# An earlier warm-up from a small cleared tile, a new order for the first four blocks, and copies moved to ScalarE

## The chip, the cores and the metric

One core of one Trainium2 chip. The metric is the device time of one execution in microseconds (us). Executions of a kernel are compared in runs of the state that the measurements call fast; the one run of 3364.69 us in the control, marked slow, is left out. What the state doesn't separate is how long TensorE ran at half clock; each run also lists its mean granted TensorE clock (the share of full speed that the chip let it run at, 1.0 or 0.5 in every record of these traces), and that turns out to matter here.

In the lines of the profile PE is TensorE, PEld its weight loads, DVE VectorE, ACT ScalarE, POOL GpSimd, and SP the queue that issues transfers (DMA). The span goes from the first to the last instruction of the profiled execution. L260 is line 260 of the kernel.

## The reference

```python
# B, H, S, D = 4, 8, 768, 48; all float32
for t in range(S):
    state = alpha[:, :, t, :, None] * state + einsum('bhd,bhde->...', k[:, :, t], v[:, :, t])   # outer product
    y[:, :, t] = einsum('bhd,bhde->bhe', q[:, :, t], state)
x = y.transpose(0, 2, 1, 3).reshape(3072, 384)
h = np.maximum(x @ w_in, 0.0)          # w_in 384 x 2048, float64 in memory
out = (h * h @ w_out).astype(np.float32)
```

(The einsum of the outer product is shortened here.) The recurrence is computed in blocks of 128 time steps: 24 blocks, four at a time as a group. A block takes logs of alpha (step `ln`), their running sums by a product with a triangle of ones (`cs`), exponentials of the sums and their inverse (`eb`, `ei`), scales q and k with them (`mq`, `mk`), turns both with TensorE (`qT`, `kT`), copies them out of PSUM, the memory that the program lets TensorE write to, in tiles called banks here (`qc`, `kc`), forms scores (`sc`), masks them (`am`), and makes outputs (`y`, `ev`) and the next state (`kv`, `st`).

## The kernel before

The steps of the first four blocks are written out in a string, in the order in which every engine gets its instructions. In the timelines each engine works through its own in that order (TensorE, before: `kT0` at 9.55 us, `qT0` at 10.02, `cs1` at 10.49, `sc0` at 11.33), so the place of a step decides what it can be held up by.

```python
    s_t = kept("s", B, [128, NP, 64])          # states, cleared by GpSimd after q and k tiles
    for t in s_t:
        nc.gpsimd.memset(t, 0.0)
    ...
    am_t = kept("am", NAM, [128, 2, NP, 128])  # masked scores, cleared by VectorE
    for t in am_t:
        nc.vector.memset(t, 0.0)
    ...
    def warm(_):
        nc.tensor.matmul(
            out=ps_att.tile([128, NP, C], FP32, tag="att", name="warm"),
            lhsT=am_t[1][:, 0, 0, :], rhs=am_t[1][:, 0], start=True, stop=True,
        )
    warm(0)
    warm(0)
    ...
    VECTOR = ("k0", "k1", "k2", "k3", "q1", "q2", )
    def copied(x, n):                          # steps kc and qc
        t = blk[n][f"{x}s"] = work(f"{x}s", 2)
        copy = nc.vector.tensor_copy if f"{x}{n}" in VECTOR else nc.scalar.copy
        copy(out=t, in_=blk[n].pop(f"{x}T"))
    ...
    first = """
        ln0 load0v warm0 cs0 ei0 eb0 mk0 mq0 load2a load2q load2k bl0 ln1 kT0 kc0 load1v
        qT0 qc0 cs1 load3a sc0 weights0 load3q load3k eb1 mq1 load2v bl1 ei1 mk1 kT1 kc1
        qT1 qc1 am0 kv0 ln2 br0 cs2 ei2 eb2 sc1 am1 mq2 bl2 load3v mk2 br1
        weights1 ln3 y0 ev0 kT2 kc2 qT2 qc2 kv1 cs3 ei3 eb3 mk3 weights2 first0 st0
        mq3 load4q load4k load4v kT3 middle0 sc2 kc3 bl3 qT3 second0 qc3 am2 br3 br2 st1
        kv2 sc3 am3 ha0 weights3 load4a ha1 first1 middle1 y2 ev2 second1 st2 hb0 first2 hb1
        kv3 middle2 st3
    """
```

`first`, `middle` and `second` are the three parts of turning a float64 weight tile into float32, on VectorE, ScalarE and VectorE. `ha` and `hb` are the first feed-forward products. Everything behind this string (the feed-forward network and the other 20 blocks) is some 535 us long and unchanged.

Of the kernel before, what the change touches and what calls it, by code (L numbers as in the profile page):

```python
# [8 lines left out]
FP32 = mybir.dt.float32  # L9
# [14 lines left out]
def kernel(  # L24
# [25 lines left out]
    nc = tc.nc  # L50
    B, H, S, D = q.shape
    C = 128
    NCH = S // C
    NP = H // 2
# [14 lines left out]
    ps_att = ctx.enter_context(tc.tile_pool(name="ps_att", bufs=4, space=PSUM))  # L69
# [4 lines left out]
    def kept(name, n, shape):  # L74
        return [consts.tile(shape, FP32, name=f"{name}{i}") for i in range(n)]

    NV = 3
    tiles = {
        "a": kept("a_in", 2, [128, H * D]), "q": kept("q_in", 2, [128, H, 64]),
        "k": kept("k_in", 4, [128, H, 64]), "v": kept("v_in", NV, [128, H * D]),  # L80
    }
# [1 line left out]
        nc.gpsimd.memset(t[:, :, D:64], 0.0)  # L83

    tiles["w"] = kept("vx_in", 2, [128, H // 2 * D])
    s_t = kept("s", B, [128, NP, 64])
    for t in s_t:
        nc.gpsimd.memset(t, 0.0)

    NW = 8  # L90
    w_in = [consts.tile([128, KM, DF // NW], FP32, name=f"w_in{i}") for i in range(NW)]
# [4 lines left out]
    def flat(t):  # L96
        return t.rearrange("a x y -> a (x y)")
# [4 lines left out]
    for n in (2, 3):  # L102
        t = lent["q", n] = flat(w_out[4 + n])[:, 0 : 64 * H].rearrange("a (h d) -> a h d", h=H)
# [104 lines left out]
    am_t = kept("am", NAM, [128, 2, NP, 128])  # L208
# [21 lines left out]

    def warm(_):
        nc.tensor.matmul(  # L232
            out=ps_att.tile([128, NP, C], FP32, tag="att", name="warm"),
            lhsT=am_t[1][:, 0, 0, :], rhs=am_t[1][:, 0], start=True, stop=True,
        )

    warm(0)
    warm(0)


    blk = [{} for _ in range(NBLK)]
# [8 lines left out]
    def work(name, bufs=1):  # L250
        return p2.tile([128, NP, C], FP32, tag=name, name=name, bufs=bufs)
# [59 lines left out]
        turned("k", n)  # L311


    VECTOR = ("k0", "k1", "k2", "k3", "q1", "q2", )

    def copied(x, n):
        t = blk[n][f"{x}s"] = work(f"{x}s", 2)
        copy = nc.vector.tensor_copy if f"{x}{n}" in VECTOR else nc.scalar.copy
        copy(out=t, in_=blk[n].pop(f"{x}T"))
# [88 lines left out]
    def y(n):  # L408
# [50 lines left out]
        for phase in range(2):  # L459
# [20 lines left out]
            for m in ns:  # L480
# [5 lines left out]
                for p in range(NP):  # L486
                    half = slice(64 * (p % 2 ^ phase), 64 * (p % 2 ^ phase) + 64)
                    for e in range(2):
# [3 lines left out]
                            lhsT=tiles["k"][m % 4][half, 2 * p + e, :],  # L492
                            rhs=tiles["v"][m % NV][half, first : first + 64],
                            start=(p % 2, e) not in begun, stop=True, skip_group_check=True,
# [209 lines left out]
    def ffn_product(g, i, r):  # L704
# [68 lines left out]
    steps["hb"] = lambda j: ffn_in(0, j, slice(HT, 2 * HT))  # L773
    steps["first"], steps["middle"], steps["second"] = convert_first, convert_middle, convert_second
    first = """
        ln0 load0v warm0 cs0 ei0 eb0 mk0 mq0 load2a load2q load2k bl0 ln1 kT0 kc0 load1v
        qT0 qc0 cs1 load3a sc0 weights0 load3q load3k eb1 mq1 load2v bl1 ei1 mk1 kT1 kc1
        qT1 qc1 am0 kv0 ln2 br0 cs2 ei2 eb2 sc1 am1 mq2 bl2 load3v mk2 br1
        weights1 ln3 y0 ev0 kT2 kc2 qT2 qc2 kv1 cs3 ei3 eb3 mk3 weights2 first0 st0
        mq3 load4q load4k load4v kT3 middle0 sc2 kc3 bl3 qT3 second0 qc3 am2 br3 br2 st1  # L780
        kv2 sc3 am3 ha0 weights3 load4a ha1 first1 middle1 y2 ev2 second1 st2 hb0 first2 hb1
        kv3 middle2 st3
    """
    for word in first.split():
        f = max((x for x in steps if word.startswith(x)), key=len)
# [97 lines left out]
```

## Time and profile before

| | before |
|---|---|
| time, three runs | 580.06, 583.12, 583.3 us |
| profiled execution | 579.81 us, span 577.9 us |
| first feed-forward product (`ha`) | 31.69 us |
| first products of full width (128x512) | 42.31 us |
| TensorE's waits, all | 9.8 us |
| clock from 20.65 to 31.69 us | 0.69 of full speed |

Read it from the back: from 42.31 us on TensorE is full, so the change can only move that moment. The lines are in the prediction.

### The profile page before, as it was taken

To read this page: it belongs to the slowest core of one execution; us is meant where nothing else is said; L and a number is where in the kernel's file an instruction comes from. 1 tells how busy PE (TensorE), PEld (TensorE's weight loads), DVE (VectorE), ACT (ScalarE), POOL (GpSimd) and SP (SyncE) were. 2 spreads that over 40 slices of the span, in tenths; PEclk is the share of its full clock that TensorE was granted. 3 is DMA by queue.
4 is the path that set the end of the run, shared out by engine and by line. 5 is a ranking of instruction groups with operands and counts; after the bars stand their busy time and mean duration, and the time that the engine had idled before them with its cause. 6 is when DMAs were issued, how large, how long until landed. Compare 5 with 4: busy or idle time off the path is not lost.

```text
span 577.9 us, 11428 instructions
## 1 busy us (share of the span) xinstructions
PE 563.1 (97%) x4754; PEld 481.8 (83%) x4754; DVE 330.1 (57%) x657; ACT 220.8 (38%) x489; POOL 4.5 (1%) x29
## 2 busy tenths in 40 slices
PE   6789999999999999999999999999999999999996
PEld 3664555677889999889999889999988999988996
DVE  3888949875784634564544565552566443366430
ACT  3457966433334423333252333342333432333100
POOL 3000000000000000000000000000000000000000
PEclk9899999999999999999999999999999999999999
DMA  9886457623001535000445100424300340100001
GB/s 165 217 194 204 110 139 230 148 33 85 0 1 30 95 59 124 1 0 14 73 85 102 37 1 1 83 57 90 77 1 1 56 68 1 56 1 1 1 1 55
DMA packets 127963, 38.94 MB, mean 67 GB/s; under 512 B 119700, under 2 KB 122792, under 8 KB 127912
## 3 DMA queue, kind: packets, MB, share of 16 engines
q1 hardware_dynamic: 127912, 38.22, 30.2%
q8 instruction: 37, 0.61, 0.4%
q14 instruction: 14, 0.11, 0.1%
HBM read 33.45 MB, written 4.75 MB: 66 GB/s over the span
## 4 chain that ended last, share of the span: by engine, by line
PE 96%; DVE 2%; issue 1%; ACT 0%; POOLq 0%
PE h L649 33%; PE o L720 32%; PE o L686 7%; PE h L611 7%; PE y L416 5%; PE cs L260 3%; PE sc L349 3%; PE kT L303 2%; PE qT L303 2%; PE kv L490 1%; PE warm L232 1%; DVE xT L514 1%; PE sc L335 1%; PE kv L393 1%; DVE am L210 0%
## 5 line engine op out<-in xcount | busy, mean ns | idle before, releaser
L649 PE MATMUL h<-xT,w_in 128*128 128x256 f32 x480 | 124.0, 379 | 0.0
L649 PEld LDWEIGHTS h<-xT,w_in 128*128 128x128 f32 x480 | 91.1, 190 | 12.4
L720 PE MATMUL o<-w_out,hid 128*128 128x192 f32 x480 | 83.3, 327 | 0.0
L720 PEld LDWEIGHTS o<-w_out,hid 128*128 128x128 f32 x480 | 78.7, 190 | 3.7
L514 ACT COPY xT<-y 32x256 f32<-32x256 f32 (+2 forms) x132 | 46.2, 365 | 79.3 <-PE y L416 73.8
L662 DVE TENSOR_TENSOR hid<-h,u 128x256 f32<-128x256 f32 x120 | 50.8, 424 | 28.8 <-PE h L649 25.0
L667 ACT ACTIVATE hid<-hid 128x256 f32<-128x256 f32 x40 | 16.7, 417 | 114.6 <-DVE hid L662 114.6
L662 DVE TENSOR_TENSOR u<-h,u 128x256 f32<-128x256 f32 x80 | 33.8, 423 | 35.3 <-PE h L649 22.9
L649 PE MATMUL h<-s3x,ws 128*128 128x256 f32 x160 | 47.6, 379 | 0.0
L384 DVE COPY_PREDICATED am<-parts,sc 128x384 f32<-128x384 uint32 x40 | 20.6, 578 | 45.2 <-PE sc L349 45.1
L611 PE MATMUL h<-xT,w_in 128*128 128x512 f32 (+1 forms) x108 | 43.7, 551 | 1.8 <-ACT xT L514 1.8
L686 PE MATMUL o<-w_out,hid 128*128 128x384 f32 x128 | 42.9, 488 | 0.0
L720 PE MATMUL o<-t,s 128*128 128x192 f32 x240 | 42.4, 328 | 0.0
L649 PE MATMUL h<-s3x,w_in 128*128 128x256 f32 x160 | 41.1, 379 | 0.0
L720 PEld LDWEIGHTS o<-t,s 128*128 128x128 f32 x240 | 39.0, 190 | 1.3
L611 PEld LDWEIGHTS h<-xT,w_in 128*128 128x128 f32 x108 | 19.7, 190 | 20.9 <-issue 16.7
L686 PEld LDWEIGHTS o<-w_out,hid 128*128 128x128 f32 x128 | 23.8, 190 | 15.6
L649 PEld LDWEIGHTS h<-s3x,w_in 128*128 128x128 f32 x160 | 30.4, 190 | 4.1
L649 PEld LDWEIGHTS h<-s3x,ws 128*128 128x128 f32 x160 | 30.4, 190 | 4.1
L720 PE MATMUL o<-t,hid 128*128 128x192 f32 x160 | 27.9, 329 | 0.0
L669 DVE SCALAR_TENSOR_TENSOR hid<-hid 128x512 f32<-128x512 f32 x40 | 27.2, 681 | 0.0
L720 PEld LDWEIGHTS o<-t,hid 128*128 128x128 f32 x160 | 25.8, 190 | 0.3
(110 smaller groups left out, 763.7 us busy)
## 6 DMA issues: line engine op xcount, KB each, us to landing
raw<-in_moe_w_in_dram SPq DMA_DIRECT2D x8, 768.0 KB, 6.6
raw<-in_moe_w_out_dram SPq DMA_DIRECT2D x8, 768.0 KB, 5.9
k_in<-in_k_dram SPq DMA_DIRECT2D x24, 192.0 KB, 4.4
out_dram<-osb SPq DMA_DIRECT2D x24, 192.0 KB, 1.9
v_in<-in_v_dram SPq DMA_DIRECT2D x23, 192.0 KB, 5.1
a_in<-in_alpha_dram SPq DMA_DIRECT2D x22, 192.0 KB, 3.6
q_in<-in_q_dram SPq DMA_DIRECT2D x22, 192.0 KB, 3.9
vx_in<-in_v_dram SPq DMA_DIRECT2D x40, 48.0 KB, 2.5
```

The source lines that it names most:

```text
L260: nc.tensor.matmul(out=ps.rearrange("a p t -> a (p t)")[:, 0 : H * D], lhsT=causal, rhs=blk[n].pop("la"), start=True, stop=True,)
L303: nc.tensor.transpose(out=ps[:, p, :], in_=rows[:, 128 * p : 128 * (p + 1)], identity=ident)
L349: nc.tensor.matmul(out=chunks(ps[e].rearrange("a p t -> a (p t)"), half, p, i), lhsT=ks[rows, p, 64 * i : 64 * (i + 1)], rhs=qs[rows, p, t ...
L384: nc.vector.copy_predicated(out=o, mask=mask.unsqueeze(1).to_broadcast(list(o.shape)), data=data)
L416: ins = nc.tensor.matmul(out=slot(ps)[64 * half : 64 * half + D + G * e, t], lhsT=lhsT, rhs=rhs, start=key not in seen, stop=True, skip_gr ...
L514: copy(out=x[to : to + m, kk, t : t + 2], in_=blk[n]["y"][e][r : r + m, :, p // 2],)
L611: nc.tensor.matmul(out=ps, lhsT=w[:, kk, c0 : c0 + 128], rhs=xT[g][:, kk, cols], start=(kk == 0), stop=(kk == KM - 1),)
L649: nc.tensor.matmul(out=ps, lhsT=a, rhs=b, start=(step.isupper() and i == 0), stop=(i == len(pairs) - 1), skip_group_check=True,)
L662: nc.vector.tensor_tensor(out=o, in0=ps, in1=z, op=ALU.add)
L669: nc.vector.scalar_tensor_tensor(out=h2, in0=h2, scalar=0.0, in1=h2, op0=ALU.max, op1=ALU.mult)
L686: nc.tensor.matmul(out=acc[t][:, 0:DM], lhsT=hid[i][:, j, t * C : (t + 1) * C], rhs=w_out[i][:, j, :], start=(i == 0 and j == 0), stop=(i ...
L720: nc.tensor.matmul(out=acc[k][:, t, :], lhsT=lhs[:, j, t * C : (t + 1) * C], rhs=rhs[:, j, :], start=(first and r + j + t == 0), stop=(r = ...
```

## The change

The intent: the zero products, among which TensorE's clock came up in the trace before (a weight load of 128 columns took 338 ns until the one at 5.78 us, and 191 from 6.62), start sooner, and a new order of the first four blocks closes gaps, with most copies of turned q and k on ScalarE (0.59 us each there in the trace before, 0.69 on VectorE).

```diff
+    s_t = kept("s", B, [128, NP, 64])         # now ahead of the q and k tiles
+    for t in s_t:
+        nc.gpsimd.memset(t, 0.0)
 ...
-            out=ps_att.tile([128, NP, C], FP32, tag="att", name="warm"),
-            lhsT=am_t[1][:, 0, 0, :], rhs=am_t[1][:, 0], start=True, stop=True,
-    warm(0)
-    warm(0)
+            out=ps_att.tile([128, NP, 64], FP32, tag="att", name="warm"),
+            lhsT=s_t[0].rearrange("a p d -> a (p d)")[:, 0:128], rhs=s_t[0], start=True, stop=True,
+    for _ in range(3):
+        warm(0)
 ...
-    VECTOR = ("k0", "k1", "k2", "k3", "q1", "q2", )
+    VECTOR = ("k1", "k2", )
 ...
+        warm0 ln0 load0v cs0 ei0 eb0 mk0 mq0 load2a load2q load2k bl0 ln1 kT0 qT0 kc0
+        load1v qc0 cs1 load3a sc0 load3k eb1 mq1 bl1 qT1 load2v ei1 mk1 weights0 kT1 kc1
+        qc1 kv0 br0 am0 load3q ln2 cs2 ei2 eb2 sc1 am1 bl2 load3v mq2 mk2 ln3
+        weights1 y0 cs3 ev0 br1 kT2 qT2 ei3 kc2 qc2 kv1 eb3 mk3 load4v kT3 first0
+        st0 mq3 weights2 load4q load4k middle0 sc2 kc3 qT3 second0 qc3 bl3 am2 br3 st1 br2
+        kv2 sc3 am3 ha0 first1 ha1 middle1 y2 ev2 load4a hb0 first2 hb1 second1 st2 kv3
+        middle2 st3 weights3
```

(The old string, printed above, is what the new one replaces.)

More of the change, by code (lines that the diff above doesn't have):

```diff
@@ L85 @@
     tiles["w"] = kept("vx_in", 2, [128, H // 2 * D])
-    s_t = kept("s", B, [128, NP, 64])
-    for t in s_t:
-        nc.gpsimd.memset(t, 0.0)
     NW = 8
@@ L775 @@
     first = """
-        ln0 load0v warm0 cs0 ei0 eb0 mk0 mq0 load2a load2q load2k bl0 ln1 kT0 kc0 load1v
-        qT0 qc0 cs1 load3a sc0 weights0 load3q load3k eb1 mq1 load2v bl1 ei1 mk1 kT1 kc1
-        qT1 qc1 am0 kv0 ln2 br0 cs2 ei2 eb2 sc1 am1 mq2 bl2 load3v mk2 br1
-        weights1 ln3 y0 ev0 kT2 kc2 qT2 qc2 kv1 cs3 ei3 eb3 mk3 weights2 first0 st0
-        mq3 load4q load4k load4v kT3 middle0 sc2 kc3 bl3 qT3 second0 qc3 am2 br3 br2 st1
-        kv2 sc3 am3 ha0 weights3 load4a ha1 first1 middle1 y2 ev2 second1 st2 hb0 first2 hb1
-        kv3 middle2 st3
+        warm0 ln0 load0v cs0 ei0 eb0 mk0 mq0 load2a load2q load2k bl0 ln1 kT0 qT0 kc0
[5 more added lines that the diff above has]
+        middle2 st3 weights3
     """
```

## The prediction

> **What bounds the kernel now.** I read the page's bars first, then the chain that ended last, then TensorE's waits, then the busy times cut at the moments where the first four blocks change stage, and last the timeline of the first 45 us.
>
> The page's bars, 40 slices of 14.4 us:
>
> ```profile
> span 577.9 us, 11428 instructions
> PE 563.1 (97%) x4754; PEld 481.8 (83%) x4754; DVE 330.1 (57%) x657; ACT 220.8 (38%) x489; POOL 4.5 (1%) x29
> ...
> PE   6789999999999999999999999999999999999996
> ...
> PEclk9899999999999999999999999999999999999999
> ...
> PE 96%; DVE 2%; issue 1%; ACT 0%; POOLq 0%
> ```
>
> TensorE is full from the fourth slice to the last, and the chain is TensorE for 96%. The feed-forward products behind it are untouched by this change. What can be won lies in slices one to three, where the bars are 6, 7 and 8 and one slice of clock shows 8. TensorE's waits are all there:
>
> ```profile
> PE warm L232 <- DVE rebias L228: 3.1, 1, 3.1
> PE kT L303 <- DVE k_in L278: 3.0, 3, 1.3
> PE h L611 <- ACT xT L514: 1.8, 3, 1.3
> PE cs L260 <- DVE ks L319: 1.7, 1, 1.7
> PE y L416 <- DVE am L371: 0.2, 1, 0.2
> ```
>
> 9.8 us in all (3.1 + 3.0 + 1.8 + 1.7 + 0.2), each column: total, times, longest. The stages, with busy times, granted clock, DMA share and GB/s:
>
> ```profile
> 0.00:9.55 9.55, 5.23 (x8) 2.11 (x9) 2.53 (x5) 3.03 (x5) 4.49 (x29) 1.00 1.06 153
> 9.55:20.65 11.10, 10.43 (x106) 8.41 (x107) 8.17 (x16) 4.01 (x11) 0.00 (x0) 1.00 1.17 205
> 20.65:31.69 11.04, 8.09 (x55) 6.56 (x54) 9.84 (x18) 4.59 (x9) 0.00 (x0) 0.69 0.95 211
> 31.69:42.31 10.62, 8.84 (x66) 6.99 (x65) 8.37 (x17) 6.76 (x16) 0.00 (x0) 1.00 0.71 187
> 42.31:577.90 535.59, 530.47 (x4526) 457.75 (x4524) 301.19 (x605) 202.44 (x451) 0.00 (x0) 1.00 0.25 58
> ```
>
> Columns are TensorE, its weight loads, VectorE, ScalarE, GpSimd. The third row is the weak one: clock 0.69 and VectorE at 9.84 of 11.04. After 42.31 nothing is left to win from this change, so its effect is the time by which 42.31 moves. Finer, the clock:
>
> ```profile
> 20.29:23.70 3.41, 1.67 (x10) 0.92 (x8) 2.81 (x6) 1.63 (x6) 0.00 (x0) 1.00 0.50 73
> 23.70:27.11 3.41, 2.20 (x14) 1.90 (x16) 2.81 (x7) 2.59 (x4) 0.00 (x0) 0.50 0.92 265
> 27.11:30.52 3.41, 3.41 (x22) 3.12 (x18) 3.38 (x5) 0.59 (x1) 0.00 (x0) 0.50 1.19 294
> ```
>
> A stretch with TensorE busy 1.67 of 3.41 us is followed by two at half clock. The start, and the late cumulative sum of block 3:
>
> ```profile
> 3.06 4.59 PE L232 MATMUL warm<-am 128*128 128x512 f32 x6 [3.06 <-DVE rebias L228]
> ...
> 7.05 0.19 PEld L260 LDWEIGHTS cs<-la,causal 128*128 128x128 f32 x1 [0.24 <-issue]
> ...
> 22.76 0.88 PE L260 MATMUL cs<-la,causal 128*128 128x384 f32 x2 [1.68 <-DVE ks L319]
> ```
>
> The warm-up products wait for VectorE's two 0.91 us clears, though they only need zeros, and the logs that the first sum needs were ready at 4.11 (ACTIVATE la, 3.59 + 0.52). The sum started at 7.48. The sum of block 3 stands behind two copies of keys on VectorE.
>
> [...] down at 23.7 after 1.67 of 3.41 us busy, up at 30.5, two windows later. The start is cold too although the clock column prints 1.00: a 128-column weight load takes 338 ns until 5.78 and 191 ns from 6.62. [...] 2 to 14 us run near 190 GB/s with the DMA engines full.
>
> **The change part by part.**
> 1. Warm-up. Three products of 128x512 become four of 128x256 on a tile that GpSimd clears first. A pass of the old form took 0.85 us cold (weight loads at 4.07, 4.93, 5.78), so a new one about 0.43, and 8 passes 3.4 us. GpSimd is free at 0.73 and clears a tile of this size in 1.06/4 = 0.27 us, so they run from about 1.1 to 4.5. The mask for the sums stays ready at 3.94, the logs at 4.11. Sum 0 starts at 4.5 rather than about 7.5, 3.0 us earlier.
> 2. Arrival. That lead meets the loads. Block 1's keys, issued at 4.69, took 5.0 us (9.7); v of block 0, issued at 5.82, 4.7 (10.5). At 196.6 KB a load and 190 GB/s, 1.03 us each, block 0's keys land about 6.1 and a of block 1 about 7.4. So: sum 4.5 to 5.2, inverse 5.7, keys scaled 6.1 to 6.65 (0.55), turned from 6.8 against 9.55; log 1 at 7.4 to 7.9, then both copies of block 0 by ScalarE (0.59 each, 0.52 apart) to 9.0, scores 0 at 9.05 against 11.33. I count 2.3 us kept here.
> 3. Blocks 0 and 1. Keys and queries of block 1: scaled 9.5 to 10.55, both turned by 11.4, the query copied by ScalarE, the key by VectorE to 12.1. kv0, then sum 2 at 12.3 (14.74 before); scores 1 to 14.1; VectorE masks block 0 in 12.1 to 13.4 and block 1 in 14.1 to 15.5. The second half of the first outputs starts about 15.5 against 18.10: 2.6 us.
> 4. Sum 3 now stands straight behind these outputs, at 16.7 against 22.76, not behind two copies. Its exponentials still come after ScalarE's six output copies (about 19.8 to 20.3); keys of block 3 are scaled by 20.9, against 24.76. With copies of block 2 split over both engines, TensorE has kT2, qT2 to 18.5, kv1 at 20.1 (it waits for the key copy to free its bank), kT3 and scores 2 to 23.0. Two shorter gaps replace 1.7 and 1.3 us with 0.9 between. If the clock stays up, kT3, scores 2, qT3 and kv2 take 0.66, 1.16, 0.60 and 1.03 rather than 1.09, 2.08, 1.11 and 1.82 us: 2.65 us less on the path.
> 5. The first weight tile is now loaded behind k3 and v2, two loads or 2.1 us later: it landed at 12.19 + 6.7 = 18.9, so now about 21.0. Its conversion began at 24.68 before, so this has slack; now it starts on landing. With st0, query 3 and three conversion passes (0.56, 0.56, 0.74, 0.56, 0.95, 0.9, 0.95 with their short waits) VectorE is done about 26.1; the first feed-forward product starts there, against 31.69: 5.5 us.
> 6. Masks 2 and 3 and st1 (1.33, 0.73, 1.34) to 29.5, outputs to 31.0, the six copies to 33.7 (2.67), then two passes for weight tile 2 that are now put ahead (1.1) and the three of tile 1 (2.8): 37.6. They ended at 42.02 before, and the full products began at 42.31. This is 4.7 us; the 0.8 lost against step 5 is the moved pair of passes, which comes back later only as slack.
>
> Four copies leave VectorE: 4 x 0.69 = 2.8 us in its busiest stage, for 4 x 0.59 = 2.4 on ScalarE, which had 4.59 of 11.04. Of this sum only 4.7 us reach the end; parts are not added to it.
>
> **The rivals.** (a) The loads set the pace: DMA engines are full from 2 us on, so the start only waits elsewhere, and about 2 us of the gain are left, 581. For it: block 1's arrivals of 9.7 and 10.5 are later than the new order could use. Against: before had 1 to 3 us of slack on each, and 20.29 to 23.70 shows share 0.50. (b) The shorter warm-up does not open the clock. Before had up to 5.1 us of cold work, the new has 3.4, just a window; with an unlucky phase the transposes and scores of block 0 and 1 run at half speed for one or two windows, 2 to 3 us back: 580 to 582. (c) The first weight tile lands late and holds VectorE, in order, before st0 and query 3: each us of delay past 21 costs one. (d) VectorE bounds the conversions behind 42 us and eats the lead: it is at 17.79 of 20 us in 40 to 60. Against: two passes have been drawn ahead, and TensorE shows only 0.2 us of waits after 40 us. All four make the time 580 to 583, none a loss of over 2%.
>
> **Range and chances.** 583.12 - 4.7 = 578.4. A chance of one in three of losing some 2 us to (a) or (b) takes off 0.7 us, while the three runs before (580.06 to 583.3) show the median may sit 3 us lower in other executions. I say 578.4, with 574.8 to 582.0 for 8 in 10. A gain of 2% is 11.7 us: more than all of TensorE's waits (9.8 us), and only possible with the clock's loss added; 2%. A loss of 2% needs a damage that no part here can do; 2%.
>
> **What would show it.** Warm-up from about 1.1 us, first scores near 9, no half-clock stretch between 20 and 31, the first feed-forward product near 26, and the first 128x512 products near 37.6, with the rest as long as before (535.6 us). Wrong if the weight loads of the first transposes take twice as long (b), if the log of block 1 or VectorE's first conversion pass waits for a DMA (a, c), or if TensorE waits for converted weights between 38 and 75 us (d).

## The result, and the profile after

The changed kernel took 575.23 us in the median of four runs (575.14 to 576.33), against 583.21 in four of the kernel before (580.06 to 583.5). The ratio is 0.9872, with a 95% interval from 0.9836 to 0.9908: within 2%, and inside the predicted range. Ratios here are the mean time of one kernel's fast runs over that of the other's of the same rounds, so not quite the ratio of the medians.

The page's bars and the chain's shares of the changed kernel:

```profile
span 573.2 us, 11429 instructions
...
PE   8789999999999999999999999999999999999996
...
PEclk9999999999999999999999999999999999999999
...
PE 96%; DVE 2%; DMA 1%; issue 0%; ACT 0%; SPq 0%; POOL 0%; POOLq 0%
```

The slice with clock 8 is gone. A new entry, DMA 1%, has come into the chain. TensorE's waits (total, times, longest):

```profile
PE h L611 <- ACT xT L514: 1.8, 3, 1.3
PE kv L393 <- DVE ks L319: 1.8, 1, 1.8
PE kT L303 <- DVE k_in L278: 1.3, 1, 1.3
PE warm L232 <- POOL s L79: 1.1, 1, 1.1
PE h L611 <- DVE am L371: 0.9, 1, 0.9
PE qT L303 <- DVE w_out L278: 0.7, 1, 0.7
PE h L611 <- DVE w_in L188: 0.6, 1, 0.6
```

With one of 0.2 they add up to 8.4 us, only 1.4 less than before: 2.0 us at the warm-up and 3.4 at the sum and the keys are saved, and new waits of 4.0 us (kv, qT and two of the feed-forward products) have come in. The rest of the span's 4.7 us is mostly busy time, 563.1 - 560.3 = 2.8 us: the warm-up is shorter and products no longer run at half clock. The stages, cut at the events that ended the stages before: keys of block 0 turned, end of the sum and the transposes of block 2, first feed-forward product, full products:

```profile
0.00:7.22 7.22, 4.86 (x11) 3.24 (x11) 2.54 (x5) 2.93 (x5) 4.47 (x29) 1.00 0.95 144
7.22:18.18 10.96, 10.73 (x102) 8.09 (x102) 7.11 (x14) 5.78 (x13) 0.00 (x0) 1.00 1.38 211
18.18:26.82 8.64, 5.28 (x58) 4.64 (x57) 7.88 (x15) 5.29 (x11) 0.00 (x0) 1.00 1.05 231
26.82:38.23 11.41, 9.01 (x65) 7.02 (x65) 9.80 (x19) 7.54 (x17) 0.00 (x0) 1.00 0.77 182
38.23:573.20 534.97, 530.43 (x4524) 458.04 (x4524) 300.26 (x604) 201.28 (x450) 0.00 (x0) 1.00 0.26 59
```

The clock column reads 1.00 in every row. (The start is still at half clock: the trace's first record of full clock begins at 5.62 us, and at 6.60 in the kernel before; the column prints 1.00 ahead of it. A weight load of 128 columns takes 338 ns at 4.67, and 190 in the sum of block 1, from 8.04.) Three lines of the timeline show where the new path runs (start, duration, engine, what; in brackets the idle time before it and what ended it):

```profile
19.95 1.13 PE L393 MATMUL kv<-v_in,k_in 128*128 128x96 f32 x8 [1.77 <-DVE ks L319]
...
21.01 0.56 DVE L159 TENSOR_SCALAR power<-raw 128x768 uint32<-128x768 uint32 x1 [0.33 <-DMA raw<-in_moe_w_in_dram]
...
26.82 2.86 PE L611 MATMUL h<-xT,w_in 128*128 128x256 f32 x12 [0.87 <-DVE am L371]
```

The conversion of the first weight tile starts when it lands, at 21.01. VectorE's next 5 us are that conversion and what stands in between, then comes the first half of a mask, and then the first feed-forward product. Against the steps of the prediction:

| moment, us | before | predicted | after |
|---|---|---|---|
| scores of block 0 | 11.33 | 9.05 | 9.01 |
| sum of block 2 | 14.74 | 12.3 | 12.03 |
| second half of the first outputs | 18.10 | 15.5 | 15.38 |
| sum of block 3 | 22.76 | 16.7 | 16.40 |
| first weight tile's conversion begins | 24.68 | 21.0 | 21.01 |
| first feed-forward product | 31.69 | 26.1 | 26.82 |
| full products | 42.31 | 37.6 | 38.23 |
| last operation of VectorE | 573.05 | | 568.93 |
| end | 577.9 | | 573.2 |

The two profiled executions are 4.1 us apart at the full products (42.31 - 38.23) and still at VectorE's last operation (573.05 - 568.93); the last 0.6 us of the 4.7 comes with the final store, between that operation and the end (4.85 and 4.27 us). The medians differ by 8.0 us, though. The experiments had to explain both numbers: which part gives what, and where the other 3 us are.

### The profile page after: what moved, and what is told of

The parts are those of the page before. It is cut to its first block, busy times and chain, and to the rows that moved or that the text cites. A ratio compares the mean times of both kernels' runs of the same rounds, so it can differ in the third digit from the quotient of the medians.

```text
span 573.2 us, 11429 instructions
## 1 busy us (share of the span) xinstructions
PE 560.3 (98%) x4756; PEld 481.0 (84%) x4756; DVE 327.6 (57%) x653; ACT 222.8 (39%) x493; POOL 4.5 (1%) x29
## 4 chain that ended last, share of the span: by engine, by line
PE 96%; DVE 2%; DMA 1%; issue 0%; ACT 0%; SPq 0%; POOL 0%; POOLq 0%
PE h L649 33%; PE o L720 32%; PE o L686 7%; PE h L611 7%; PE y L416 5%; PE cs L260 3%; PE sc L349 3%; PE qT L303 2%; PE kT L303 2%; PE kv L490 1%; DMA raw<-in_moe_w_in_dram 1%; PE warm L232 1%; PE sc L335 0%; DVE xT L514 0%; PE kv L393 0%
## 5 line engine op out<-in xcount | busy, mean ns | idle before, releaser
L649 PEld LDWEIGHTS h<-xT,w_in 128*128 128x128 f32 x480 | 91.1, 190 | 12.3
L667 ACT ACTIVATE hid<-hid 128x256 f32<-128x256 f32 x40 | 16.7, 417 | 114.6 <-DVE hid L662 114.6
```

Source lines behind the costliest of these rows:

```text
L649: nc.tensor.matmul(out=ps, lhsT=a, rhs=b, start=(step.isupper() and i == 0), stop=(i == len(pairs) - 1), skip_group_check=True,)
```

## The experiments

Two theories. Theory A, the prediction's: a shorter start and one half-clock stretch avoided make some 4.7 us, and that the runs before lie between 580 and 583.5 is chance of the chip. Theory B: the kernel before usually loses more to half clock than its profiled execution did, how much depending on the phase of the clock's windows, and a good part of the gain is that this has become rare. All twelve runs gave a correct result. They ran in four jobs on three chips; the kernel before ran along in each, 164 times in all.

### The kernel before, again

No edit.

> The unchanged kernel, as a control and to see its clock in another execution. Theory A (the gain is 4.7 us by a shorter first stretch, and the other 3 us between 580 and 583.3 is chance of the chip): ratio 1.000, the profile shows one half-clock stretch near 24 to 30.5 us again, and the first feed-forward product near 31.7 us. Theory B (the usual execution of this kernel has a longer or a second half-clock stretch that the profiled one was spared, by another phase of the clock's window): where a run takes 583 us, its mean granted clock is lower than 0.993 and the first full products start near 45 rather than 42.3 us.

Measured: ratio 1.0003, median 583.64, the profiled execution at 583.55 us. The times are not spread, they come in groups, and the groups go with the clock. The 164 runs of the kernel before (the 21 fast ones of this control lie in the same groups and are not counted in):

| mean clock | runs | mean time |
|---|---|---|
| 0.987 to 0.988 | 98 | 583.8 |
| 0.989 | 2 | 581.6 |
| 0.993 | 49 | 579.5 |
| 0.994 | 15 | 581.1 |

The profile on which the prediction rests is of the 0.993 group, less than a third of the runs. This profile is of the usual one; the stretches here are cut at the moments where its clock changes:

```profile
21.48:24.89 3.41, 1.08 (x4) 0.33 (x3) 2.34 (x6) 1.77 (x6) 0.00 (x0) 1.00 0.75 123
24.89:28.30 3.41, 2.79 (x20) 2.49 (x20) 3.32 (x8) 2.00 (x3) 0.00 (x0) 0.50 0.99 342
28.30:31.72 3.42, 3.42 (x20) 3.02 (x20) 3.38 (x5) 0.58 (x1) 0.00 (x0) 0.50 1.38 222
31.72:35.13 3.41, 3.41 (x21) 2.83 (x20) 2.91 (x7) 0.00 (x0) 0.00 (x0) 0.50 0.32 40
...
38.54:41.95 3.41, 1.77 (x12) 0.71 (x7) 2.81 (x7) 2.98 (x8) 0.00 (x0) 1.00 1.09 353
41.95:45.37 3.42, 3.28 (x8) 2.66 (x9) 3.32 (x6) 0.89 (x3) 0.00 (x0) 0.50 1.41 200
```

Each row is one window of about 3.41 us; the first number behind the comma is TensorE's busy time, and the third from the end its clock. Two windows with little work (1.08 and 1.77 us of it) are each followed by half clock: three windows, then one more, four in all where the first profile had two. The full products began at 46.39 us. Theory B holds for the kernel before: the 4 us between its runs are half-clock windows, not chance of the chip.

### One part alone

Warm-up alone (`warm_only`: the early clear and the short zero products, old string, old copies), order alone (`order_only`: the new string, the rest old), copies alone (`copies_only`):

```diff
-    VECTOR = ("k0", "k1", "k2", "k3", "q1", "q2", )
+    VECTOR = ("k1", "k2", )
```

> Only the warm-up is changed: four short products on a tile cleared first, old order, old copies. Theory A (start and half-clock stretch are separate gains): the first sum starts near 4.6 instead of 7.5 us, about 2 us of it are kept at the first feed-forward product (29.7 instead of 31.7), the gap before the sum of block 3 and the half-clock stretch stay; ratio 0.996 to 0.997. Rival (loads set the pace): less than 0.7 us is kept, ratio 0.999 or more.

> Only the order of the steps is changed: old warm-up, all six copies on VectorE. Theory A: no half-clock stretch between 20 and 31 us, first feed-forward product near 28.7 instead of 31.7 us, full products near 39.8 instead of 42.3; ratio 0.994 to 0.996. Rival (the copies must be moved for the order to pay): VectorE is later by its four copies, 2.8 us, gain under 1 us, ratio 0.998 or more.

> Only four copies of turned q and k go from VectorE to ScalarE, old order and warm-up. Theory A: VectorE is not what the sum of block 3 waits for once the query copy of block 2 is gone: 0.7 us earlier there, half-clock stretch perhaps shorter; ratio 0.997 to 0.9995. Rival (copies make the whole gain by freeing VectorE in its busiest stage): 2.8 us or more, ratio 0.995 or less.

| kernel | ratio (95%) | runs | at clock 0.990 or less | mean of runs at 0.998 or more |
|---|---|---|---|---|
| warm_only | 0.9956 (0.9936 to 0.9976) | 20 | 12 | 576.8 (1 run) |
| order_only | 0.9962 (0.9946 to 0.9978) | 22 | 11 | 579.0 (7 runs) |
| copies_only | 0.9991 (0.9970 to 1.0012) | 22 | 11 | none |

The warm-up gives what Theory A said: the first sum at 4.67 us, and the first feed-forward product at 30.19 against 33.24 in the control of the same clock, 3.05 us earlier where about 2 were expected. Between runs of the same clock it is 2.7 us (583.8 - 581.1 at 0.988). The half-clock stretch stays, as expected. For the order, the ratio was within what was expected of it and the mechanism was not: its profile has three half-clock windows, after one with 1.62 us of work (cut at the changes of the clock).

```profile
20.74:24.15 3.41, 1.62 (x13) 1.39 (x12) 3.33 (x8) 2.14 (x7) 0.00 (x0) 1.00 0.91 251
24.15:27.57 3.42, 3.42 (x25) 3.07 (x23) 3.33 (x7) 1.76 (x3) 0.00 (x0) 0.50 0.67 111
27.57:30.98 3.41, 3.41 (x23) 3.03 (x22) 3.34 (x6) 0.45 (x1) 0.00 (x0) 0.50 1.12 294
30.98:34.39 3.41, 3.41 (x10) 2.77 (x9) 2.31 (x5) 0.40 (x2) 0.00 (x0) 0.50 0.35 31
```

So the new order alone doesn't keep the clock up. The copies alone can't be told from nothing.

### One part taken back

`no_warm` has the old warm-up with new order and copies, `no_copies` the old copies with the rest new, `no_order` the old string with the rest new. `after_again` is the changed kernel as it is.

> The changed kernel once more, for the spread of its time and clock. Theory B (the kernel before loses 2 to 4 windows of 3.41 us at half clock, how many depends on the window's phase; the changed one has too few gaps for that): nearly all runs within 575 to 576.5 us, hardly any at a clock of 0.988. Theory A (the spread is chance of the chip): a spread of some 4 us here too, with a third of the runs above 578.

> The changed kernel with the old warm-up: new order and moved copies alone. Theory B with copies and order together closing the gaps: the clock stays up at nearly all phases, so only the start's 2.6 us are missing: 577.7 to 578.3, ratio 0.990 to 0.992, more than order_only (0.9962) and copies_only (0.9991) together. Additive rival: 0.9953, about 580.

> The changed kernel with its copies back on VectorE: new warm-up and order. Theory B: as in order_only the gaps before the keys of block 3 and the scores of block 2 are too long and the half-clock stretch comes in most runs: 577 to 578, ratio 0.9905 to 0.992, with runs from 575.5 to 579.5. Rival (copies matter only by 0.1%): 575.8, ratio 0.9875.

> The changed kernel with the old order: new warm-up and moved copies. Theory B: the gap before the sum of block 3 stays, two to four half-clock windows: 579 to 580.5, ratio 0.993 to 0.996, with a spread of 4 us. Rival (order matters little): 577 or less.

| kernel | ratio (95%) | mean | runs | at clock 0.990 or less | mean of runs at 0.995 or more |
|---|---|---|---|---|---|
| after_again | 0.9886 (0.9849 to 0.9922) | 575.7 | 6 | 0 | 575.7 |
| no_warm | 0.9937 (0.9914 to 0.9960) | 578.6 | 16 | 4 | 577.7 |
| no_copies | 0.9903 (0.9869 to 0.9937) | 577.1 | 7 | 2 | 576.3 |
| no_order | 0.9963 (0.9941 to 0.9984) | 580.2 | 22 | 16 | 577.0 (1 run) |

With the first four, ten runs of the changed kernel lie between 574.9 and 576.5, none with a clock below 0.995. Taking the order back costs most, 4.5 us (580.2 - 575.7), and there 16 of 22 runs are at low clock. Without the warm-up the median (577.77) is as expected and the ratio is not, because four runs of 16 have fallen to 581. Order and copies together (`no_warm`) give 0.63%, and 0.38% and 0.09% alone. That they need each other is not shown by this: the additive rival's ratio, 0.9953, lies inside the interval. I take the split by clock below as the stronger sign. `no_copies` was expected to fall to half clock in most runs; two of seven did.

The profile of `no_warm` has a half-clock window (24.79 to 28.20 us), and its execution took 577.81 us, no longer than the five runs at 0.999 (577.73 in the mean). Its first feed-forward product did not wait for VectorE's masks, as that of the changed kernel does (0.87 us). So one window at half clock there cost nothing.

### Idle products in the gaps of the kernel before

To part the clock from everything else, the old kernel got products of a zero tile in TensorE's gaps, and no other edit:

```diff
+    def fill(_):
+        nc.tensor.matmul(
+            out=ps_ffn.tile([128, NP, 64], FP32, tag="f", name="fill"),
+            lhsT=s_t[3].rearrange("a p d -> a (p d)")[:, 0:128], rhs=s_t[3], start=True, stop=True,
+        )
-  ... qT2 qc2 kv1 cs3 ei3 eb3 ...        ... y2 ev2 second1 ...
+  ... qT2 qc2 kv1 fill0 fill0 fill0 cs3 fill0 fill0 ei3 eb3 ...        ... y2 fill0 fill0 ev2 second1 ...
```

> The kernel before with seven idle products of a zero tile put into TensorE's gaps (three and two around the sum of block 3, two behind the outputs of blocks 2 and 3), nothing else moved. Theory B (half-clock windows are most of the gain): the clock stays at 0.998 or more in nearly all runs, the spread of 4 us goes, and 577 to 578.5 us come out without any of the change: ratio 0.990 to 0.993, profile without a half-clock stretch. Rival (VectorE is as late without the half clock, so the path goes through it): 581 to 583, ratio 0.998 or more, clock up all the same.

Measured: ratio 0.9968 (0.9948 to 0.9988), mean 580.45. No run has a clock of 0.990 or less, where 100 of the 164 runs without the fill have. Ten of 22 runs, at 0.999 or 1.000, take 579.1 us in the mean. That is the old schedule (with seven products more) at full clock, and it is only 0.4 us below the 0.993 group. I had expected 577 to 578.5, and a clock of 0.998 or more in nearly all runs. The wait ahead of the first feed-forward product shows why (lines are shifted by 6 in this kernel):

```profile
PE h L617 <- DVE am L377: 1.5, 1, 1.5
```

TensorE, at full clock, only came sooner to a wait for VectorE's masks: the first feed-forward product started at 31.18 us instead of 31.69. The other 12 runs, at a clock of 0.996, take 581.6. None of them was profiled, so where they lose 2.5 us is open.

### The sum of block 3 put back

```diff
-        weights1 y0 cs3 ev0 br1 kT2 qT2 ei3 kc2 qc2 kv1 eb3 mk3 load4v kT3 first0
+        weights1 y0 ev0 br1 kT2 qT2 kc2 qc2 kv1 cs3 ei3 eb3 mk3 load4v kT3 first0
```

> The changed kernel with the sum of block 3 put back behind the copies of block 2, as before, all else new. Theory B with the place of this sum as the part that keeps the clock: half-clock windows in most runs, first full products 41 to 44 instead of 38.2 us, 577.5 to 580.5, ratio 0.992 to 0.996. Rival (the moved copies alone shorten the gap enough): 576 to 577, clock above 0.997.

Measured: ratio 0.9944 (0.9922 to 0.9966), mean 578.5, 10 of 21 runs at 0.990 or less. Its profile has two half-clock windows from 22 us on and full products from 40.76 us. Seven runs at 0.995 or more take 576.3, 0.7 us more than the changed kernel. So the place of this one sum is worth little by itself; what it does for the other 2.2 us of the mean (578.5 - 576.3) is keep the clock. Of all stretches of 3.41 us that start between 8 and 40 us, the one with the least work of TensorE holds 0.88 us of it with the sum at the back (from 18.5 us, as in the kernel before from 21.25), and in the changed kernel two hold 1.64 and 1.63 (from 16.75 and 31.5).

### Two attempts at a faster kernel

`better` loads the first weight tile ahead of v of block 2, and puts the state of block 0 behind the tile's conversion:

```diff
-        load1v qc0 cs1 load3a sc0 load3k eb1 mq1 bl1 qT1 load2v ei1 mk1 weights0 kT1 kc1
+        load1v qc0 cs1 load3a sc0 load3k eb1 mq1 bl1 qT1 weights0 ei1 mk1 load2v kT1 kc1
-        st0 mq3 weights2 load4q load4k middle0 sc2 kc3 qT3 second0 qc3 bl3 am2 br3 st1 br2
+        mq3 weights2 load4q load4k middle0 sc2 kc3 qT3 second0 st0 qc3 bl3 am2 br3 st1 br2
```

> The changed kernel with the first weight tile loaded ahead of v of block 2 and the state of block 0 made after the conversion of that tile rather than within it. If the first tile's landing and its conversion on VectorE set the time of the first feed-forward product, as the chain of the changed kernel says: that product 0.7 to 1.0 us earlier (25.9 instead of 26.8), total 574.5 to 575, ratio 0.9855 to 0.987. Rival (the masks and outputs of blocks 2 and 3 end the wait anyway, as they come after on VectorE): first product earlier, full products at 38.2 as they were, 575.5.

Measured: ratio 0.9896 (0.9856 to 0.9936), six runs from 574.84 to 578.92, so not faster than the changed kernel. The slowest run is at a clock of 0.988: the new schedule isn't proof against half clock, it meets it seldom. The profiled execution shows something else. The same line in the changed kernel and then in this one, the transposes of block 0's keys:

```profile
7.22 0.63 PE L303 MATMUL kT<-ident,k_in 128*128 128x128 f32 x4 [1.26 <-DVE k_in L278]
```

```profile
7.42 1.09 PE L303 MATMUL kT<-ident,k_in 128*128 128x128 f32 x4 [1.26 <-DVE k_in L278]
```

Here the four short zero products didn't open the clock in time. The transposes took 1.09 us rather than 0.63, the scores of block 0 started at 10.57 rather than 9.01, and the span is 574.6 rather than 573.2. From these scores to the first feed-forward product it is 17.57 us (28.14 - 10.57), against 17.81 in the changed kernel: the rearrangement saves 0.2 us, where 0.7 to 1.0 was expected, because that product waits for VectorE's masks (0.8 us) as it does after the change.

`better_fill` adds idle products, to keep the clock up without delaying anything:

```diff
-        warm0 ln0 load0v cs0 ei0 ...   kT2 qT2 ei3 ...   y2 ev2 load4a ...
+        warm0 ln0 load0v cs0 fill0 ei0 ...   kT2 qT2 fill0 fill0 fill0 ei3 ...   y2 fill0 fill0 ev2 load4a ...
```

> The changed kernel with the small rearrangement of the run called better, plus six products of a zero tile in TensorE's remaining gaps: one behind the first sum, three ahead of kv of block 1, two behind the outputs of blocks 2 and 3. Theory B: what still spreads the changed kernel (574.9 to 576.5, once 578.9 in better) is the phase of the clock, at the start and now and then later; with the gaps filled every run is at a clock of 0.999 or more and between 574.5 and 575.5, ratio 0.986 to 0.988. Rival (the spread has another cause, or idle products delay the real ones): 575.7 or more with the same spread.

Measured: ratio 0.9884 (0.9843 to 0.9925), and six runs between 574.66 and 575.57, mean 575.0, all at 0.998 or more. The ten runs of the changed kernel have a mean of 575.6. It is the tightest of all kernels here and has the lowest time; that it is faster than the changed kernel by 0.6 us is likely but not shown, with six runs on another chip. The ratio says less than these times do, because the kernel before had six of its 11 runs of this job in its two faster groups.

## Why the prediction was right

**The time.** 575.23 us lies in 574.8 to 582.0 but near its lower end, 3.2 us below the 578.4 predicted. The step that is off is the starting point. The prediction took 4.7 us from a profile and the time from the median of three runs, and put down their 3.2 us of difference to executions that may be luckier. By their times they were runs of two clock groups: 583.12 and 583.3 of the one with four half-clock windows, 580.06 and the profiled 579.81 of the one with two. The kernel before should have been seen as a mixture, with what the change takes from each group. That the result still lies in the range is luck in part: the range was drawn 3 us downward for executions luckier than the median of before, while in fact that median was the usual group and the change gained 8.0 us from it, not 4.7.

**Steps 1 to 3, start and arrival.** Right to 0.3 us at the moments of the table. Inside them the first sum was put down as 0.7 us and took 1.28, since the clock rose only at 5.62 us, and the keys of block 0 were turned at 7.22 instead of 6.8; the copies by ScalarE, put down from 7.9 on, still began at 7.88. Rival (a), loads setting the pace, kept nothing from the gain there, but the first weight tile did become the thing waited for at 21.01 (rival c): its chain share of 1% and the 0.33 us wait say so. At full clock the warm-up is worth 577.7 - 575.6 = 2.1 us at the end, of the 2.3 said to be kept at the first scores.

**Step 4, the clock.** The half-clock stretch went, as predicted, but not because both gaps became shorter: the one before `kv` of block 1 is 1.77 us, as long as the 1.68 before the old sum, and only the other shrank (0.72 against 1.27). What the order changed is the least work that TensorE has in any 3.41 us, 1.63 us instead of 0.88. The size was wrong in both ways. In an execution with two half-clock windows, 2.65 us were to come off the path. The filled kernel shows 0.4 us (579.5 - 579.1), since VectorE's masks are next. In the usual execution with four such windows it is 4.7 us (583.8 - 579.1), which the prediction didn't have. As a mean over all 164 runs (582.3) half clock costs 3.2 us, and the ten changed runs (575.6) are 6.7 us faster. The gain is so about half clock (3.2) and half schedule (3.5: 2.1 of it the warm-up, 1.4 order and copies together, 579.1 - 577.7). These are estimates from differences of group means, and they take the ten best runs of the filled kernel for the old schedule at full clock.

**Step 5.** The conversion began when predicted (21.0), but the first feed-forward product came at 26.82 instead of 26.1. The step left out a wait: its PSUM bank, from the four of the feed-forward pool, is still held by a score tile of block 2 until VectorE has masked it. The trace names that mask (0.87 us). (The step's own parts add up to 26.2 rather than 26.1, and its gain to 5.6 rather than 5.5.) In the kernel before TensorE was too late to meet it, as the filled kernel confirms.

**Step 6.** Right by difference: 11.41 us from there to the full products, 11.5 predicted. It ended 0.6 late for step 5's reason.

**Rivals.** (b), the shorter warm-up that doesn't open the clock, happened in one profiled execution (`better`), at 1.6 us, a little under the 2 to 3 predicted. (d), conversions bounding what follows, did not happen: 534.97 us from the full products to the end, against 535.59. TensorE waited once for converted weights (0.62 us), and that wait ended at 38.23: it is the conversion with which step 6 ends, at 37.6.

**What stays open.** Why the changed kernel met half clock so seldom. The clock's changes in the 14 traces lie whole multiples of 3.413 us apart (in the first profile of the kernel before 6.60, 23.67 and 30.50 us, five and two of them), so each trace gives away its own windows. Eleven windows at full clock with 0.88 to 1.94 us of TensorE's work were followed by half clock, in the first 55 us; of those that were not, one held 1.89 us and no other less than 2.03. The changed kernel has stretches of 3.41 us with only 1.63 and 1.64 us of work, but in its two profiles no window lay on them: the least held 2.10 us.

```profile
5.62:9.03 3.41, 2.10 (x13) 1.13 (x12) 1.03 (x2) 2.50 (x6) 0.00 (x0) 1.00 1.46 182
29.51:32.93 3.42, 2.12 (x34) 1.77 (x33) 2.02 (x5) 3.06 (x6) 0.00 (x0) 1.00 0.30 25
```

If the windows are slid over the trace of the changed kernel and it is otherwise left as it is, 61% of their positions catch a stretch with less than 1.85 us. This is an estimate, with a limit chosen after the falls had been seen. For `no_warm` it gives 60%, and 11 of 16 runs had a clock under 0.998; for `order_only` 61%, and 15 of 22 had; for the two traces of the kernel before 100% and 95%, and all 164 had. Of the ten changed runs only one had (at 0.995, and it lost no time). So the windows' position was kind to the changed kernel, by chance or for a reason that the runs don't show, and the 3.2 us that it owes to the clock may be fewer elsewhere; `better_fill`, whose profile has no stretch under 2.40 us between 8 and 40 us, should not depend on it (an estimate: no window with more than 1.94 us of work was followed by half clock). One full window did not always bring the clock back: in the second profile of the kernel before, the one from 28.30 to 31.72 us (3.42 us busy) was followed by another at half clock, and only the next full one by full clock. Four of the 14 profiles have six such windows, and what decides it is not shown. Nor do the runs show where the 0.994 group of the kernel before loses its time.

## What to carry to other kernels

List the runs of a kernel by their clock before believing a single profile: a median of two groups and the profile of one of them can't be compared. In a stretch where TensorE waits a lot, a gap can cost twice, once itself and again as half clock for some windows behind it (here nothing for one window, about 0.4 us for two and 4.7 for four, as other waits took up the rest); moving one small product forward into a gap, or a zero product into it, is a cheap test of that. And before counting what a faster engine will save, look which wait stands next, including for a bank.
